# One level of Strassen for the first channel product of batches 5 to 7 and of the tail chunk

## The chip, the cores and the metric

The kernel runs on one core of one Trainium2 chip. Its time is the device time of one execution in microseconds (us); the median of three executions stands for it. A profile of one more execution shows what each engine did: TensorE (PE, and PEld for its weight loads), VectorE (DVE), ScalarE (ACT), GpSimd (POOL) and SyncE (SP), which here only issues transfers.

## The reference

The program is attention with random features, followed by a mixer with a token part and a channel part. Cut to its sums, for 8 batches, 8 heads, 576 tokens and 64 values per head:

```python
q_p, k_p = phi(q * scale), phi(k * scale)      # 128 features, exp of a projection
kv  = einsum('bhsm,bhsd->bhmd', k_p, v)
num = einsum('bhsm,bhmd->bhsd', q_p, kv)       # divided by the sum of the features
x   = attention as (8, 576, 512)
u   = x + (relu(x^T @ w_tok1) @ w_tok2)^T      # 576 -> 256 -> 576 tokens
out = u + relu(u @ w_ch1) @ w_ch2              # 512 -> 1536 -> 512 channels
```

The change concerns `u @ w_ch1`, called here the first channel product. `relu(...) @ w_ch2` is the second.

## The kernel before, in words

Of each batch the first 512 tokens are one chunk; the last 64 tokens of all eight batches are gathered into a ninth chunk, the tail, which is chunk number 8 in the code. For each batch the kernel loads q, k and v (from batch 2 on through a copy in DRAM and a transposing transfer on SP's queue), forms the features, the attention output `x`, and in the token part `u`. A transposing transfer then brings `u` into the layout `uT`, in which the channels lie on the partitions.

The channel part of a chunk is `channel_mix`. Its first product has 12 blocks of 128 hidden channels. For each, four matmuls of 512 columns (L966) sum over the 512 input channels in one of the eight PSUM banks, and one instruction, on ScalarE or VectorE, applies relu and writes `r3` as 16-bit floats (`relu_to`, L290 on ScalarE, L292 on VectorE). The second product is done from chunk 1 on by one level of Strassen's algorithm, in `channel_out_fast`: VectorE forms eight sums of quarters of `r3` (the tile `S`, `tt` at L295), TensorE computes seven products of 12 matmuls of 256 columns (L916) into three banks X, Y and Z that go on accumulating, and after each product VectorE reads a bank out and adds it to `u` or to what it read before (`read`, L905). Each of the seven products waits for the relus of all 12 blocks. The tail's second product is done in two halves, so that the last reads and stores are small.

The work is recorded as jobs with an engine, a planner's cost, dependencies, and buffers that they take and give back. `Planner.run` does not plan: it issues the jobs in an order written out in `ORDER`, with buffer places from `SLOT`, and `MOVED` overrides a job's usual engine by its number. So each engine's instructions stand in the sequence in which `ORDER` names them, and an instruction that must wait holds up all behind it on its engine. `engine(usual)` looks a job up in `MOVED`. The helper that applies a relu knows two engines:

```python
def relu_to(eng, out, in_):
    if eng == "ACT":
        nc.scalar.activation(out=out, in_=in_, func=AF.Relu)
    else:
        nc.vector.tensor_relu(out=out, in_=in_)
```

while `tt`, for sums of two tiles, has a branch for GpSimd. Rings of buffers: three each for transposed q, transposed k, v and `uT`, four each for the features `qp` and `kp`, two for `r3`, one for `S`, eight PSUM banks.

Of the kernel before, what the change touches and what calls it, by code (L numbers as in the profile page):

```python
# [81 lines left out]
]  # L82
SLOT = (
    "0100234050607011034025217063304156020014123024233037016112506321174115613214067030406102530471612141"
    "6710324016307250311067345122353640751421105324100325261073641220501046112501420700521173142350120702"
    "6123534100753141200127003221065413207102503410160022357312126034171542176210025011041121126022037516"
# [82 lines left out]
def kernel(  # L169
# [27 lines left out]
    R = SM // 2  # L197
    RT = ST // 2
    RA = R + RT
    NPE = 2  # L200
    RW = S * 4 // P
    c_scale = float(1.0 / math.sqrt(math.sqrt(D)))

# [93 lines left out]
    def bank(name):  # L297
        return banks[place("bank", name)]
# [772 lines left out]
```

## Time and profile before

| | us |
|---|---|
| median of the runs | 277.35 |
| lowest and highest | 276.93, 278.52 |
| span of the profiled execution, first to last instruction | 275.9 |
| TensorE busy in that span | 266.6 |
| VectorE busy | 222.9 |
| ScalarE busy | 138.1 |
| GpSimd busy | 91.2 |

The span leaves out what lies around the first and the last instruction, so the median stands 1.45 us above it. A row of a group shows line, engine, operation, output and input, shapes and count, then busy time and mean duration, then idle time before the group and what ended it. Instructions of one engine overlap a little in such rows: what a queue pays for an instruction is the distance between the starts of two that follow each other directly.

### The profile page before, as it was taken

To read this page: it belongs to the slowest core of one execution; us is meant where nothing else is said; L and a number is where in the kernel's file an instruction comes from. 1 tells how busy PE (TensorE), PEld (TensorE's weight loads), DVE (VectorE), ACT (ScalarE), POOL (GpSimd) and SP (SyncE) were. 2 spreads that over 40 slices of the span, in tenths; PEclk is the share of its full clock that TensorE was granted. 3 is DMA by queue.
4 is the path that set the end of the run, shared out by engine and by line. 5 is a ranking of instruction groups with operands and counts; after the bars stand their busy time and mean duration, and the time that the engine had idled before them with its cause. 6 is when DMAs were issued, how large, how long until landed. Compare 5 with 4: busy or idle time off the path is not lost.

```text
span 275.9 us, 6228 instructions
## 1 busy us (share of the span) xinstructions
PE 266.6 (97%) x2503; PEld 165.5 (60%) x2503; DVE 222.9 (81%) x462; ACT 138.1 (50%) x289; POOL 91.2 (33%) x115
## 2 busy tenths in 40 slices
PE   8789999999999999999999999999999999999993
PEld 3367455444567655755676656755676477446782
DVE  3897889876998799987999899978985992675992
ACT  3999941188685338734756456636654500040200
POOL 8994492063703490075019510600043000000001
PEclk9999999999999999999999999999999999999998
DMA  7999999999998999979989994840252304021125
GB/s 195 192 209 212 190 212 177 202 193 146 203 191 133 229 176 186 151 148 171 198 184 183 232 125 123 191 90 2 97 79 77 96 0 95 2 99 53 78 83 146
DMA packets 81292, 39.66 MB, mean 144 GB/s; under 512 B 63984, under 2 KB 77040, under 8 KB 81072
## 3 DMA queue, kind: packets, MB, share of 16 engines
q0 software_dynamic: 31744, 17.74, 44.2%
q1 hardware_dynamic: 47072, 15.50, 28.7%
q10 hardware_dynamic: 2448, 6.03, 5.6%
q8 instruction: 19, 0.31, 0.5%
q14 instruction: 9, 0.07, 0.1%
HBM read 35.95 MB, written 16.52 MB: 190 GB/s over the span
## 4 chain that ended last, share of the span: by engine, by line
PE 89%; DMA 6%; POOL 3%; DVE 0%; issue 0%; POOLq 0%
PE bank L966 33%; PE bank L916 25%; PE bank L777 5%; PE bank L790 5%; DMA w1m<-in_moe_w_tok_dram 4%; PE bank L1000 4%; PE bank L734 3%; PE bank L656 3%; PE bank L668 2%; PE bank L701 2%; DMA uT<-u 2%; POOL r L319 1%; PE bank L844 1%; PE bank L816 1%; PE bank L828 1%; PE bank L736 1%
## 5 line engine op out<-in xcount | busy, mean ns | idle before, releaser
L966 PE MATMUL bank<-uT,wc 128*128 128x512 f16 x376 | 90.4, 379 | 0.3 <-DMA uT<-u 0.3
L290 ACT ACTIVATE r<-bank 128x512 f16<-128x512 f32 (+1 forms) x84 | 46.9, 597 | 77.1 <-PE bank L966 62.0
L295 POOL TENSOR_TENSOR vs<-v,vs 128x512 f16<-128x512 f16 x31 | 33.2, 1074 | 91.2 <-DVE vs L682 60.5
L966 PEld LDWEIGHTS <-wc 128*128 128x128 f16 x424 | 38.3, 98 | 37.9 <-issue 1.1
L916 PEld LDWEIGHTS <-r 128*128 128x128 f16 x384 | 36.9, 98 | 8.1 <-issue 1.2
L514 ACT ACTIVATE kp<-bank 128x512 f16<-128x512 f32 x64 | 35.6, 622 | 10.4 <-PE bank L656 10.4
L514 ACT ACTIVATE qp<-bank 128x512 f16<-128x512 f32 x64 | 36.3, 616 | 8.9 <-PE bank L668 6.0
L680 DVE TENSOR_REDUCE km<-kp 128x8 f16<-128x1024 f16 x32 | 38.6, 1206 | 2.5 <-ACT kp L514 2.4
L292 DVE TENSOR_SCALAR r<-bank 128x512 f16<-128x512 f32 (+1 forms) x42 | 27.7, 672 | 12.0 <-PE bank L966 11.2
L744 DVE TENSOR_TENSOR x<-bank,rc 128x320 f16<-128x320 f32 x62 | 30.5, 492 | 2.1
L916 PEld LDWEIGHTS <-S 128*128 128x128 f16 x288 | 27.9, 98 | 5.4 <-issue 0.3
L905 DVE TENSOR_TENSOR o<-u,bank 128x512 f32<-128x512 f16 x28 | 19.0, 679 | 6.9 <-PE bank L916 6.8
L916 PE MATMUL bank<-T,r 128*128 128x256 f16 x192 | 23.8, 273 | 0.0
L916 PE MATMUL bank<-T,S 128*128 128x256 f16 x192 | 23.6, 273 | 0.0
L916 PE MATMUL bank<-wc,r 128*128 128x256 f16 x192 | 23.6, 273 | 0.0
L945 POOL DMA_DIRECT2D out_dram<-o x2 | 1.3, 648 | 60.9 <-issue 60.9
L793 DVE TENSOR_TENSOR u<-x,bank 128x512 f16<-128x512 f16 x28 | 17.8, 681 | 1.1 <-PE bank L790 1.0
L905 DVE TENSOR_TENSOR o<-o,bank 128x512 f32<-128x512 f32 (+1 forms) x27 | 16.6, 618 | 2.2 <-PE bank L916 1.6
L734 PEld LDWEIGHTS <-qp 128*128 128x128 f16 x256 | 13.8, 98 | 7.0 <-DVE kvsb L286 0.2
L734 PE MATMUL bank<-kvsb,qp 128*128 128x65 f16 x256 | 15.6, 193 | 0.0
L743 DVE RECIPROCAL rc<-bank 128x5 f32<-128x5 f32 x62 | 11.5, 186 | 4.1 <-PE bank L736 2.7
L701 PEld LDWEIGHTS <-kp 128*128 128x128 f16 x256 | 11.5, 98 | 5.1
(120 smaller groups left out, 376.3 us busy)
## 6 DMA issues: line engine op xcount, KB each, us to landing
out_dram<-o ACTq DMA_DIRECT2D x9, 512.0 KB, 2.6
q<-in_q_dram POOLq DMA_DIRECT2D x6, 576.0 KB, 7.2
wc<-in_moe_w_ch_dram POOLq DMA_DIRECT2D x4, 768.0 KB, 10.6
k<-in_k_dram POOLq DMA_DIRECT2D x6, 512.0 KB, 6.9
v<-in_v_dram POOLq DMA_DIRECT2D x6, 512.0 KB, 8.9
out_dram<-o SPq DMA_DIRECT2D x5, 512.0 KB, 3.9
r<-in_q_dram POOLq DMA_DIRECT2D x4, 288.0 KB, 7.3
v<-in_v_dram POOLq DMA_DIRECT2D x4, 256.0 KB, 8.7
```

The lines of the kernel that those rows point to most:

```text
L290: nc.scalar.activation(out=out, in_=in_, func=AF.Relu)
L292: nc.vector.tensor_relu(out=out, in_=in_)
L295: (nc.gpsimd if eng == "POOL" else nc.vector).tensor_tensor(**kw)
L514: nc.scalar.activation(out=out, in_=in_, func=AF.Exp, bias=0.0, scale=1.0)
L680: nc.vector.reduce_max(out=mx, in_=kpv, axis=AX.X)
L701: nc.tensor.matmul(ps[:, i, :], kpv[:, 2 * i + j // 2, j % 2, :], vs[:, i * NJ + j, 0 : D + 1], start=(i == 0 and j == 0), stop=False, ski ...
L734: nc.tensor.matmul(ps[:, k, j * 65 : (j + 1) * 65], st, s[:, i, 0 : D + 1], start=True, stop=True)
L744: nc.vector.tensor_tensor(out=t_x[place("x", b)][:, :, (2 * hp + hs[0]) * D : (2 * hp + hs[0] + n) * D].rearrange("p j (i d) -> p i j d", ...
L793: nc.vector.tensor_tensor(out=t_u[place("u", b)][:, j, :], in0=t_x[place("x", b)][:, j, :], in1=bank(n), op=ALU.add)
L905: nc.vector.tensor_tensor(out=o, in0=a, in1=ps, op=ALU.add)
L916: nc.tensor.matmul(ps[:, j * DH : (j + 1) * DH], a[:, cb, j * P : (j + 1) * P], w[:, cb, :], start=(bank_of(b, j0) not in held and j == j0 ...
L966: nc.tensor.matmul(ps, wc1[:, db, cb * P : (cb + 1) * P], moving(db), start=(db == 0), stop=(db == ND - 1))
```

## The change

For chunks 5, 6, 7 and 8 (`FAST_IN = 5`) `channel_in_fast` replaces the 12 blocks of the first product. The product is taken as 2 x 2 blocks (hidden channels by tokens, over two halves of the input channels) and computed by seven block products instead of eight. In three passes (`m` = 0, 1, 2), each over a third of the hidden channels, there are seven products of four matmuls of 256 columns in three banks:

- Once for all chunks, four sums of quarters of `w_ch1` (`weight_sums`, on GpSimd), kept in two places of the ring of transposed q and two of the ring of transposed k.
- Once per chunk, four differences of quarters of `uT` (on VectorE), kept in a place of the ring for v.
- In each pass: P1, P2 and P5 start banks X, Y and Z. ScalarE keeps the state of X three times (`keep`, a copy to 32-bit floats in a place of the `qp` or `kp` ring), between P1 and P6, P6 and P7, P7 and P4. VectorE adds a kept state to bank Y or Z three times (`join`, into `r3`). Three of the four blocks need relu after that: one instruction for two of them, `relu1` on 1024 values per partition, one for the third, `relu22` on 512 values, both in place in `r3`; the fourth is applied while bank X is read out (`relu21`).

`ORDER`, `SLOT` and `MOVED` are new. The sequence of real work is the same up to the second product of batch 2 (its product number 5), and all engines' sequences differ from there on; ahead of it only a few filler matmuls on zeros and the places of buffers differ. `MOVED` names GpSimd for eleven of the new relus (six `relu1`, five `relu22`). `relu_to` is unchanged, and in the built program none of them stands in GpSimd's sequence: these eleven stand in VectorE's, each at its place in `ORDER`.

```diff
+    def weight_sums(key):
+        def quad(i, k):
+            return wc1[:, 2 * k : 2 * k + 2, i * (DC // 2) : (i + 1) * (DC // 2)]
+        steps = ((quad(1, 0), quad(1, 1), ALU.add), (0, quad(0, 0), ALU.subtract), (quad(0, 0), quad(1, 0), ALU.subtract), (quad(0, 1), 1, ALU.subtract))
+        for i, (a, b, op) in enumerate(steps):
+            e_sum = engine("POOL")
...
+    def channel_in_fast(c, key, jt):
...
+        steps = ((lambda: block(0, 1), lambda: block(0, 0)), (lambda: block(1, 1), lambda: sums()[:, 0]), (lambda: block(1, 1), lambda: block(0, 1)),
+                 (lambda: block(1, 0), lambda: sums()[:, 1]))
...
+            def product(what, deps, m=m):
...
+                    for n in range(2):
+                        for a in range(2):
+                            nc.tensor.matmul(ps[:, n, :], w_[:, a, (2 * m + n) * P : (2 * m + n + 1) * P], x_[:, a],
+                                             start=(what in ("P1", "P2", "P5") and n == 0 and a == 0), stop=False, skip_group_check=True)
...
+            def keep(what, b, dep, m=m):
+                e_keep = engine("ACT")
+                def go(what=what, b=b, e_keep=e_keep, m=m, c=c):
+                    copy(e_keep, kept(what, m), bank(bank_of(b, m)))
...
+            def join(what, b, i, j, deps, free, m=m):
+                def go(what=what, b=b, i=i, j=j, m=m, c=c):
+                    nc.vector.tensor_tensor(out=r3(i, j, m), in0=kept(what, m).rearrange("p (n t) -> p n t", n=2), in1=pair(b, m), op=ALU.add)
...
+            p1 = product("P1", [])
+            p2 = product("P2", [])
+            p5 = product("P5", [])
+            k1 = keep("P1", "X", p1)
+            c11 = join("P1", "Y", 0, 0, [k1, p2], True)
+            p6 = product("P6", [k1])
+            k2 = keep("U2", "X", p6)
+            p7 = product("P7", [k2])
+            k3 = keep("U3", "X", p7)
+            c22 = join("U3", "Z", 1, 1, [k3, p5], False)
+            p3 = product("P3", [c22])
+            c12 = join("U2", "Z", 0, 1, [k2, p3], True)
+            p4 = product("P4", [k3])
+            e_relu = engine("ACT")
+            def relu21(e_relu=e_relu, m=m, c=c):
+                relu_to(e_relu, r3(1, 0, m), pair("X", m))
...
+            e_relu = engine("DVE")
+            def relu1(e_relu=e_relu, m=m, c=c):
+                t = t_r3[place("r3", c)][:, 2 * m : 2 * m + 2, :]
+                relu_to(e_relu, t, t)
...
+            e_relu = engine("DVE")
+            def relu22(e_relu=e_relu, m=m, c=c):
+                relu_to(e_relu, r3(1, 1, m), r3(1, 1, m))
...
     def channel_mix(c, key, jt):
...
+        if c >= FAST_IN:
+            channel_out_fast(c, key, channel_in_fast(c, key, jt))
+            return
...
+        if b == FAST_IN:
+            weight_sums(b - 1.0)
         channel_mix(b, float(b), uT)
```

More of the change, by code (lines that the diff above doesn't have):

```diff
@@ L100 @@
[L100 to L103 removed]
+    44: "ACT", 48: "ACT", 53: "ACT", 61: "ACT", 64: "ACT", 67: "ACT", 68: "ACT", 114: "DVE", 116: "ACT",
@@ L104 @@
+    857: "ACT", 858: "POOL", 873: "POOL", 874: "POOL", 897: "ACT", 1003: "ACT", 1004: "POOL", 1019: "POOL",
+    1020: "ACT", 1035: "POOL", 1036: "ACT", 1059: "ACT", 1060: "ACT", 1166: "DVE", 1168: "POOL", 1182: "DVE",
+    1184: "ACT", 1199: "POOL", 1200: "ACT", 1223: "ACT", 1224: "ACT", 1247: "POOL", 1248: "ACT", 1264: "ACT",
+    1278: "DVE", 1279: "ACT", 1280: "POOL", 1318: "SP", 1323: "ACT", 1324: "SP", 1325: "ACT", 1326: "SP",
 }
@@ L200 @@
     NPE = 2
+    FAST_IN = 5
     RW = S * 4 // P
@@ L865, in channel_out_fast @@
             part = slice(g * NH // 2, (g + 1) * NH // 2)
-            need = [jr[cb + NH * e] for cb in range(part.start, part.stop) for e in range(2)]
+            need = [x for cb in range(part.start, part.stop) for e in range(2) for x in jr[cb + NH * e]]
             steps = (
@@ L953, in channel_out_fast, with sum_of, go @@
             dma(eng, key + 0.9 + 0.1 * i, 1.3, store, deps=[outs[x, 0] for x in need], give=[("o", (c, i))], cost=0.4)
+    j_sums = []
+    def sum_of(i):
+        return (t_qT if i < 2 else t_kT)[place("qT" if i < 2 else "kT", ("sum", i))][:, 0 : 2 * DC // 2].rearrange("p (a c) -> p a c", a=2)
+    def weight_sums(key):
[4 more added lines that the diff above has]
+            e_sum = engine("POOL")
+            def go(i=i, a=a, b=b, op=op, e_sum=e_sum):
+                a, b = [sum_of(x) if isinstance(x, int) else x for x in (a, b)]
+                tt(e_sum, out=sum_of(i), in0=a, in1=b, op=op)
+            need = [j_sums[x] for x in (a, b) if isinstance(x, int)]
+            j_sums.append(add(e_sum, 3.0, key, go, deps=[*need, *j_wc1], take=[("qT" if i < 2 else "kT", ("sum", i))]))
@@ new lines, in channel_in_fast, with block, sums, go @@
+    def channel_in_fast(c, key, jt):
+        def block(k, j):
+            return (t_uT[place("uT", c)] if c < B else uTt)[:, 2 * j : 2 * j + 2, 2 * k : 2 * k + 2, :].rearrange("p j a t -> p a j t")
+        def sums():
+            return t_v[place("v", ("sums", c))].rearrange("p h e -> p (h e)").rearrange("p (i a j t) -> p i a j t", i=4, a=2, j=2)
+        steps = ((lambda: block(0, 1), lambda: block(0, 0)), (lambda: block(1, 1), lambda: sums()[:, 0]), (lambda: block(1, 1), lambda: block(0, 1)),
+                 (lambda: block(1, 0), lambda: sums()[:, 1]))
+        j_s = []
+        for i, (a, b) in enumerate(steps):
+            e_sum = engine("DVE")
+            def go(i=i, a=a, b=b, e_sum=e_sum, c=c):
+                tt(e_sum, out=sums()[:, i], in0=a(), in1=b(), op=ALU.subtract)
+            j_s.append(add(e_sum, 0.35, key, go, deps=[*jt, *([j_s[i // 2]] if i % 2 else [])], take=[("v", ("sums", c))]))
+        half_c = DC // 2
+        def weights(i, k):
+            return lambda: wc1[:, 2 * k : 2 * k + 2, i * half_c : (i + 1) * half_c]
+        ops = {
+            "P1": ("X", weights(0, 0), lambda: block(0, 0), []),
+            "P2": ("Y", weights(0, 1), lambda: block(1, 0), []),
+            "P5": ("Z", lambda: sum_of(0), lambda: sums()[:, 0], [j_sums[0], j_s[0]]),
+            "P6": ("X", lambda: sum_of(1), lambda: sums()[:, 1], [j_sums[1], j_s[1]]),
+            "P7": ("X", lambda: sum_of(2), lambda: sums()[:, 2], [j_sums[2], j_s[2]]),
+            "P4": ("X", weights(1, 1), lambda: sums()[:, 3], [j_s[3]]),
+            "P3": ("Z", lambda: sum_of(3), lambda: block(1, 1), [j_sums[3]]),
+        }
+        jr = [[] for _ in range(NCB)]
+        for m in range(NH // 2):
+            kk = key + 0.5 * m / 3
+            def bank_of(b, m=m):
+                return ("in" + b, c, m)
+            def pair(b, m=m):
+                return bank(bank_of(b, m)).rearrange("p (n t) -> p n t", n=2)
+            def product(what, deps, m=m):
+                b, w, x, need = ops[what]
+                used = [("qT" if i < 2 else "kT", ("sum", i)) for i in range(4) if what == ("P5", "P6", "P7", "P3")[i]]
+                def go(b=b, w=w, x=x, what=what, m=m, c=c):
+                    ps, w_, x_ = pair(b, m), w(), x()
+                    for n in range(2):
+                        for a in range(2):
+                            nc.tensor.matmul(ps[:, n, :], w_[:, a, (2 * m + n) * P : (2 * m + n + 1) * P], x_[:, a],
+                                             start=(what in ("P1", "P2", "P5") and n == 0 and a == 0), stop=False, skip_group_check=True)
+                j = add("PE", mm(4, 256), kk, go, deps=[*need, *jt, *j_wc1, *deps], take=[("bank", bank_of(b))], give=[("v", ("sums", c)), *used] + ([("uT", c)] if c < B else []))
+                j.heavy = True
+                return j
+            def part(what, m=m):
+                tag = "qp" if (what == "U2") == (m % 2 == 0) else "kp"
+                return tag, (what, c, m)
+            def kept(what, m=m):
+                tag, name = part(what, m)
+                t = t_qp[place(tag, name)].rearrange("p a b -> p (a b)") if tag == "qp" else t_kp[place(tag, name)].rearrange("p a b e -> p (a b e)")
+                return t.bitcast(FP32)
+            def keep(what, b, dep, m=m):
+                e_keep = engine("ACT")
+                def go(what=what, b=b, e_keep=e_keep, m=m, c=c):
+                    copy(e_keep, kept(what, m), bank(bank_of(b, m)))
+                return add(e_keep, 0.5, kk, go, deps=[dep], take=[part(what)])
+            def r3(i, j, m=m):
+                return t_r3[place("r3", c)][:, NH * i + 2 * m : NH * i + 2 * m + 2, 2 * P * j : 2 * P * j + 2 * P]
+            def join(what, b, i, j, deps, free, m=m):
+                def go(what=what, b=b, i=i, j=j, m=m, c=c):
+                    nc.vector.tensor_tensor(out=r3(i, j, m), in0=kept(what, m).rearrange("p (n t) -> p n t", n=2), in1=pair(b, m), op=ALU.add)
+                return add("DVE", 0.6, kk, go, deps=deps, take=[("r3", c)], give=[part(what)] + ([("bank", bank_of(b))] if free else []))
+            p1 = product("P1", [])
[14 more added lines that the diff above has]
+                relu_to(e_relu, r3(1, 0, m), pair("X", m))
+            c21 = add(e_relu, 0.5, kk, relu21, deps=[p4], take=[("r3", c)], give=[("bank", bank_of("X"))])
+            e_relu = engine("DVE")
+            def relu1(e_relu=e_relu, m=m, c=c):
+                t = t_r3[place("r3", c)][:, 2 * m : 2 * m + 2, :]
+                relu_to(e_relu, t, t)
+            c1 = add(e_relu, 0.35, kk, relu1, deps=[c11, c12], take=[("r3", c)])
+            e_relu = engine("DVE")
+            def relu22(e_relu=e_relu, m=m, c=c):
+                relu_to(e_relu, r3(1, 1, m), r3(1, 1, m))
+            c2 = add(e_relu, 0.2, kk, relu22, deps=[c22], take=[("r3", c)])
+            for n in range(2):
+                jr[2 * m + n] = [c1]
+                jr[NH + 2 * m + n] = [c21, c2]
+        return jr
@@ L984, in relu @@
                 relu_to(e_relu, t_r3[place("r3", c)][:, cb, :], bank(n))
-            jr[cb] = (add(e_relu, 0.5, key + 0.5 * pos / NCB, relu, deps=[j1], take=[("r3", c)], give=[("bank", n)]))
+            jr[cb] = [add(e_relu, 0.5, key + 0.5 * pos / NCB, relu, deps=[j1], take=[("r3", c)], give=[("bank", n)])]
         if fast:
@@ L1001, in channel_mix @@
                 prev = add("PE", mm(4, 512) + (mm(4, P) if part == 2 else 0.0), key + 0.5 + 0.5 * (3 * j + part) / 12, c2,
-                           deps=[prev, *jr[4 * part : 4 * part + 4], *j_wc2], take=[("bank", n)], give=[("r3", c), ("uT", c)])
+                           deps=[prev, *(x for done in jr[4 * part : 4 * part + 4] for x in done), *j_wc2], take=[("bank", n)], give=[("r3", c), ("uT", c)])
             k2 = key + 0.5 + 0.5 * (3 * j + 3) / 12
```

33 lines of the change are left out of this document (14 added, 19 removed), and 123 rows, old and new, of the table ORDER.

## The prediction

> **What bounds the kernel now.** I read the page first, then the chain of waits in order of time, then busy time by stretches.
>
> ```profile
> span 275.9 us, 6228 instructions
> ...
> PE 266.6 (97%) x2503; PEld 165.5 (60%) x2503; DVE 222.9 (81%) x462; ACT 138.1 (50%) x289; POOL 91.2 (33%) x115
> ...
> PE 89%; DMA 6%; POOL 3%; DVE 0%; issue 0%; POOLq 0%
> ```
>
> The chain is TensorE for 89% of the span, and VectorE for 0% of it, though VectorE is the second busiest. In the chain by time, the stretch that the new order covers begins with the second product of batch 2, at 131.39:
>
> ```profile
> 131.39 1.31 PE bank L916 x12
> ...
> 234.09 13.81 PE bank L966 x64
> ...
> 260.94 10.51 PE bank L916 x96
> 271.48 0.42 DVE o L905
> ```
>
> A matmul of 512 columns costs 13.81/64 = 0.216 us, one of 256 columns 10.51/96 = 0.1095. After the last of them there remain VectorE's last read, to 271.90, and 4.0 us of stores, to 275.9. By stretches (columns: PE, PEld, DVE, ACT, POOL busy, then clock and transfers):
>
> ```profile
> 131.40:271.90 140.50, 140.04 (x1202) 91.37 (x1200) 114.86 (x232) 56.78 (x114) 23.55 (x26) 1.00 0.50 105
> 131.40:160.00 28.60, 28.60 (x289) 18.72 (x288) 26.24 (x57) 16.61 (x35) 11.76 (x14) 1.00 1.08 195
> 160.00:190.00 30.00, 30.00 (x275) 18.21 (x274) 27.22 (x56) 16.33 (x33) 5.29 (x6) 1.00 0.62 117
> 219.00:248.00 29.00, 29.00 (x179) 17.16 (x178) 19.12 (x33) 5.04 (x10) 0.00 (x0) 1.00 0.17 43
> ```
>
> TensorE has no gap at full clock. VectorE is busy 114.86 of 140.5 us, so it has 25.6 us to spare; in the first two rows only about 2.5 of 29. This spare time is what the change spends.
>
> **TensorE's part.** Per chunk 48 x 0.216 = 10.36 us become 7 products x 3 passes x 4 matmuls x 0.1095 = 9.20. That is 1.16 us less, for four chunks 4.7 us. If all else stays hidden, the span is 271.2.
>
> **VectorE's part.** Prices per instruction are distances between starts:
>
> ```profile
> L292 DVE TENSOR_SCALAR r<-bank 128x512 f16<-128x512 f32 x23 | 15.4, 686 | 8.8 <-PE bank L966 8.5
> ```
> ```profile
> 210.15 0.68 DVE L905 TENSOR_TENSOR o<-o,bank 128x512 f32<-128x512 f32 x1
> 210.75 0.68 DVE L905 TENSOR_TENSOR o<-u,bank 128x512 f32<-128x512 f16 x1
> ```
> ```profile
> 104.28 0.55 DVE L295 TENSOR_TENSOR S<-r 128x768 f16<-128x768 f16 x1
> ...
> 107.47 0.55 DVE L295 TENSOR_TENSOR S<-S,r 128x768 f16<-128x768 f16 x1
> ```
> ```profile
> 48.17 0.95 DVE L448 TENSOR_TENSOR T<-wc 128x1536 f16<-128x1536 f16 x1
> 49.04 0.95 DVE L448 TENSOR_TENSOR T<-wc,T 128x1536 f16<-128x1536 f16 x1
> ```
>
> ```profile
> 265.87 0.41 DVE L905 TENSOR_TENSOR o<-ut,bank 128x256 f32<-128x256 f16 x1
> 266.20 0.41 DVE L905 TENSOR_TENSOR o<-o,bank 128x256 f32<-128x256 f32 x1
> ```
>
> An instruction that reads 512 values from a bank costs 0.60 (210.15 to 210.75), one that reads 256 costs 0.33 (265.87 to 266.20). The six steps from 104.28 to 107.47 give 0.53 for a sum of 768 16-bit values, at best 0.47; 1536 values cost 0.87. From 0.47 and 0.87: 0.52 ns per value and 0.07 us fixed, so 0.34 for 512 values and 0.60 for 1024.
>
> Out go 22 of the 23 relus from banks that VectorE does in this stretch: 22 x 0.60 = 13.2. In come 36 joins (a bank of 512 plus 512 32-bit values, the form of the row at 210.15): 36 x 0.60 = 21.6. Sixteen differences of `uT`, 512 values: 16 x 0.34 = 5.4. Three `relu21` from a bank: 1.8. Nine `relu1` of 1024 values and five `relu22` of 512, eleven of these fourteen being those that `MOVED` gives to GpSimd and `relu_to` issues on VectorE. A relu inside SBUF has no row. Upper end: the price of a sum of two tiles, 0.60 and 0.34. Lower end: the fixed part and half of the rest, 0.34 and 0.20. I take 0.52 and 0.33, nearer the upper end, whose rows are nearest: 6.3 in all, between 4.1 and 7.1. The sum: 114.9 - 13.2 + 21.6 + 5.4 + 1.8 + 6.3 = 136.8 us (134.6 to 137.6), against 140.5 - 4.7 = 135.8 for TensorE. The spare time is gone, and VectorE becomes the longer engine of the stretch.
>
> By the tier table in the Trainium skill's "VectorE: DVE Perf Modes" (The perf-mode tier table), a 16-bit single-source instruction inside SBUF runs at four values per cycle, a sum of two tiles at two. With that page's errata formula, an estimate is 0.33 us for `relu1` and 0.19 for `relu22`; VectorE's sum would be 134.4, and the time below 278.8 instead of 280.0 (four and three of them lie ahead of the point that counts). No run here shows such an instruction yet.
>
> **The other engines.**
>
> ```profile
> 101.66 2.63 ACT L290 ACTIVATE r<-bank 128x512 f16<-128x512 f32 x5 [4.29 <-PE bank L966]
> ```
> ```profile
> L295 POOL TENSOR_TENSOR vs<-v,vs 128x512 f16<-128x512 f16 x31 | 33.2, 1074 | 91.2 <-DVE vs L682 60.5 <-PE bank L668 22.3 <-PE bank L966 4.5
> ...
> L295 POOL TENSOR_TENSOR T<-vt,T 128x1024 f16<-128x1024 f16 x1 | 1.9, 1941 | 0.0
> ```
>
> ScalarE pays (2.63 - 0.60)/4 = 0.51 per bank. It gets 36 keeps (18.4) and 19 new relus, three of them on 1024 values (about 11.2), and loses 26 (13.3): 56.8 + 16.3 = 73 of 140, not a bound. GpSimd: 0.87 us per 512 values more, so 2.8 for a sum of 1536; four make 11.2, and 23.6 becomes 35. They stand in front of its multiplications for batches 6 and 7; `kv` of batch 6 comes some 10 us after the third sum in TensorE's order, so that cover holds. Cost: nothing.
>
> Transfers: two of the three places for transposed q now hold sums, so batch 7's q loads only when batch 6's is used up, and on SP it stands behind a store of batch 4.
>
> ```profile
> uT<-u SPq DMA_TRANSPOSE x7, 5.4
> ...
> qT<-q SPq DMA_TRANSPOSE x6, 6.1
> ```
>
> By my count of the sequences it lands 1 us before TensorE needs it. Cost nothing, no more cover than that.
>
> **On the path.** I follow the new sequences from 131.4. Batch 6's second product waits for all relus of its first; the last is a `relu1` on VectorE. Behind it in VectorE's order stand 18 joins (10.8), 24 sums S (12.7), 14 reads of 0.60 (8.4), 14 half reads of 0.33 (4.6), 8 differences (2.7), 10 relus (5.1) and an addition (0.6): 44.9. So ahead of it are 136.8 - 44.9 = 91.9. VectorE also waits ahead of it: about 0.5 for batch 5's `uT` (5.4 us after the last addition to `u`), 0.5 at the start, and 1.4 where P5, join, P3, join follow each other across two engines (P3 alone is 4 x 0.1095 = 0.44, and three times VectorE has nothing ready beside it): 2.4, an estimate from walking through the two sequences side by side with these prices; its ends are 0 and 5. TensorE is free about 1.7 us before the relu ends and waits.
>
> Behind the relu TensorE has seven products of 1.31 (9.2), 42 first products of batch 7 and the tail at 0.44 (18.4), seven of 1.31 for batch 7 (9.2) and 84 matmuls for the tail (9.2): 46.0. There it waits about 2.0 more: 0.5 for the five relus in a row on VectorE ahead of batch 7's second product, 0.8 for that one's sums S (with a `relu22` just ahead of them), 0.7 around the tail, whose seven joins and three relus follow each other on VectorE.
>
> Sum: 131.4 + 91.9 + 2.4 + 0.1 (hand-over) + 46.0 + 2.0 = 273.8 for the last matmul; 0.2 until its result can be read, 0.45 for the read (271.45 to 271.90 before) and 4.0 for the stores give a span of 278.5, 2.6 more than 275.9. The median of the runs stood 1.45 above that span: 277.35 + 2.6 = **280.0 us**.
>
> **The rivals.**
> 1. Faster: VectorE runs without a gap. VectorE's spare time so far (25.6 us) speaks for buffers that let it run ahead. Against it: joins sit between matmuls in both directions. With no waits at all, the span is 278.5 - 4.4 = 274.1, the median 275.6; with the lower price of the relus (1.1 less ahead of batch 6's last relu) 274.5. It decides once the waits fall below 0.4 us, or 1.5 with cheap relus.
> 2. No change: half of the waits. 280.0 - 2.2 = 277.8; with cheap relus 276.7. VectorE then gives back just what TensorE saves.
> 3. Slower still: GpSimd's sums of 1536 values hold up VectorE's sums of two tiles. One of them can meet each of the S sums or the differences for up to 2.8 us, and VectorE has nothing left to hide that; one or two such meetings give 282.8 to 285.6. In the rows from 219 on GpSimd has no sum at all, so the trace doesn't decide it. The Trainium skill's "SBUF — State Buffer" (SBUF: two separate sides) states such a rule: a VectorE instruction with two SBUF inputs and a GpSimd one that reads SBUF lock a shared pair of ports for the whole instruction. No run here shows it.
>
> **How the numbers follow.** No change means within 0.5%, 1.4 us, about what a measurement of this kernel can tell. Chances: rival 1 0.12, rival 2 0.25, the forecast (278.7 to 282) 0.43, rival 3 0.20. So faster 0.12, same 0.25, slower 0.63. The range leaves out most of rival 1 and the upper part of rival 3: 275.8 to 284; slower cases alone: 278.7 to 285.6.
>
> **What would show it.** In the new profile, between 131 and 272 us: VectorE's busy time near 137 us against 115; TensorE's near 136 with gaps, which end on joins, relus or reads by VectorE; VectorE in the chain with some per cent, where it had 0%. A `relu1` lasting 0.35 us instead of 0.6 would show rival 2's price. A VectorE sum that lasts 1 us or more beside a GpSimd sum shows rival 3. The prediction is wrong if TensorE stays without gaps behind batch 5, which needs VectorE to run joins well ahead of need, or if TensorE waits at batch 7's q.

## The result and the profile after

The changed kernel takes 289.12 us (median; 288.40 to 292.81), the kernel before in the same runs 277.3: the ratio is 1.0421, with an interval of 1.0396 to 1.0445. The forecast was 280.0, with a range of 275.8 to 284.0. The sign was right, the size was not: 11.8 us more instead of 2.6. An execution more than 1.5% above the fastest of its kernel and at a lower clock, like the one of 292.81 us here, counts in the medians but not in the ratios, so differences between variants of the change are taken from the ratios below (1% is 2.8 us). The profile shown here is of one more execution, which took 288.34 us at a span of 286.6. Its page, then its busy time by stretches (columns as before: PE, PEld, DVE, ACT, POOL, then clock, share of the transfers, GB/s):

```profile
span 286.6 us, 6599 instructions
...
PE 268.8 (94%) x2647; PEld 182.0 (64%) x2647; DVE 247.0 (86%) x506; ACT 155.9 (54%) x321; POOL 104.5 (36%) x119
...
PE 57%; DVE 20%; DMA 9%; issue 7%; POOL 3%; ACT 2%; POOLq 0%; DVEq 0%
```
```profile
131.00:160.00 29.00, 27.33 (x304) 18.09 (x302) 25.52 (x55) 19.75 (x41) 16.93 (x15) 1.00 1.12 198
160.00:190.00 30.00, 24.77 (x219) 17.04 (x216) 27.43 (x46) 14.14 (x29) 12.59 (x9) 0.89 0.42 75
190.00:220.00 30.00, 29.08 (x300) 22.09 (x298) 29.29 (x58) 18.83 (x38) 5.83 (x5) 1.00 0.32 78
```

VectorE is now in the chain with 20%, and between 190 and 220 us it is busy 29.29 of 30 us: this is what was forecast. What was not forecast lies in the first two rows. Between 160 and 190 us TensorE is busy for 24.77 us only, at a granted clock of 0.89. Its waits from 128 us on (total, times, longest), and its rows around the first of the seven products of batch 4's second channel product:

```profile
PE bank L922 <- DVE r L298: 5.3, 2, 4.6
PE bank L557 <- DMA kT<-k: 1.7, 1, 1.7
```
```profile
169.92 0.62 PE L850 MATMUL bank<-r,w 128*64 128x512 f16 x4 [0.31 <-DVE u L799]
175.19 2.72 PE L922 MATMUL bank<-wc,r 128*128 128x256 f16 x12 [4.65 <-DVE r L298]
177.70 0.64 PE L707 MATMUL bank<-vs,kp 128*128 128x65 f16 x8
...
180.57 0.29 PE L740 MATMUL bank<-kvsb,qp 128*128 128x65 f16 x4
```

Three losses stand here. TensorE waits 1.67 us at 141.90 for transposed k of batch 6. It waits 4.65 us for batch 4's last relu. And behind that its first 12 matmuls take 2.51 us (175.19 to 177.70) where 1.31 is the price at full clock. Why the relu is late is seen in VectorE's rows ahead of it and GpSimd's rows beside them:

```profile
161.93 2.61 DVE L599 TENSOR_TENSOR vbd<-rct,mask 128x8 f16<-128x8 f16 x1
...
169.78 1.39 DVE L301 TENSOR_TENSOR S<-r 128x768 f16<-128x768 f16 x1
171.21 3.32 DVE L301 TENSOR_TENSOR r<-r 128x768 f16<-128x768 f16 x1
174.46 0.68 DVE L298 TENSOR_SCALAR r<-bank 128x512 f16<-128x512 f32 x1
```
```profile
160.36 3.11 POOL L301 TENSOR_TENSOR kT<-wc,qT 128x1536 f16<-128x1536 f16 x1
163.43 1.06 POOL L301 TENSOR_TENSOR vs<-v,vs 128x512 f16<-128x512 f16 x1
...
167.68 3.08 POOL L301 TENSOR_TENSOR vs<-v,vs 128x512 f16<-128x512 f16 x3 [1.37 <-DVE vs L688]
170.72 3.40 POOL L301 TENSOR_TENSOR kT<-wc 128x1536 f16<-128x1536 f16 x1
```

A product of 8 values per partition lasts 2.61 us beside GpSimd's third sum and the multiplication behind it (0.20 us elsewhere); a sum of two tiles lasts 3.32 us beside the fourth sum, another 1.39 beside three multiplications (0.55 elsewhere). Together that is some 6 us, and it is the sign that the prediction named for rival 3. VectorE's reduces and its reads of banks between them keep their times. GpSimd's first two sums, at 152.39 and 155.58, meet no VectorE instruction on two tiles, and nothing is late there.

In the kernels below the list of jobs takes another number of lines, so that the same line has another number: L301 (L295 in the kernel before) is L286 in most variants of the changed kernel and L281 in those of the kernel before.

### The profile page after: what moved, and what is told of

The parts are those of the page before. It is cut to its first block, busy times and chain, and to the rows that moved or that the text cites. A ratio compares the mean times of both kernels' runs of the same rounds, so it can differ in the third digit from the quotient of the medians.

```text
span 291.0 us, 6599 instructions
## 1 busy us (share of the span) xinstructions
PE 271.0 (93%) x2647; PEld 183.2 (63%) x2647; DVE 249.1 (86%) x506; ACT 155.8 (54%) x321; POOL 104.6 (36%) x119
## 4 chain that ended last, share of the span: by engine, by line
PE 58%; DVE 21%; issue 8%; DMA 5%; ACT 5%; POOL 0%; POOLq 0%; DVEq 0%
PE bank L1086 14%; PE bank L922 14%; PE bank L1018 7%; PE bank L1120 4%; DMA kT<-k 3%; DVE km L686 3%; DVE S L301 3%; DVE r L1039 3%; DVE o L911 3%; PE bank L707 2%; PE bank L740 2%; DVE u L799 2%; PE bank L783 2%; DMA uT<-u 2%; PE bank L662 2%
## 5 line engine op out<-in xcount | busy, mean ns | idle before, releaser
L301 POOL TENSOR_TENSOR vs<-v,vs 128x512 f16<-128x512 f16 x31 | 33.1, 1072 | 79.9 <-DVE vs L688 40.0
L1086 PE MATMUL bank<-uT,wc 128*128 128x512 f16 x232 | 56.2, 379 | 1.8 <-DVE o L911 1.8
L296 ACT ACTIVATE r<-bank 128x512 f16<-128x512 f32 (+1 forms) x67 | 38.1, 596 | 34.5 <-PE bank L1086 19.0
L922 PEld LDWEIGHTS <-r 128*128 128x128 f16 x384 | 37.7, 100 | 15.2 <-issue 7.4
L1086 PEld LDWEIGHTS <-wc 128*128 128x128 f16 x232 | 20.9, 98 | 22.3 <-issue 3.1
L922 PE MATMUL bank<-wc,r 128*128 128x256 f16 x192 | 25.7, 290 | 4.9 <-DVE r L298 4.5
L922 PE MATMUL bank<-T,S 128*128 128x256 f16 x192 | 24.9, 282 | 0.5 <-DVE o L911 0.3
L292 ACT CAST kvsb<-bank 128x130 f16<-128x130 f32 x23 | 6.7, 293 | 22.1 <-PE bank L714 18.7
L292 ACT COPY qp<-bank 128x512 f32<-128x512 f32 x16 | 9.4, 587 | 15.8 <-PE bank L1018 11.0
L292 ACT COPY kp<-bank 128x512 f32<-128x512 f32 x20 | 11.0, 594 | 12.5 <-PE bank L1018 12.5
L298 DVE TENSOR_SCALAR r<-bank 128x512 f16<-128x512 f32 (+1 forms) x23 | 15.0, 659 | 3.1 <-PE bank L1086 2.6
## 6 DMA issues: line engine op xcount, KB each, us to landing
wc<-in_moe_w_ch_dram POOLq DMA_DIRECT2D x4, 768.0 KB, 11.2
```

The source lines that it names most:

```text
L292: (nc.scalar.copy if eng == "ACT" else nc.vector.tensor_copy)(out=out, in_=in_)
L301: (nc.gpsimd if eng == "POOL" else nc.vector).tensor_tensor(**kw)
L922: nc.tensor.matmul(ps[:, j * DH : (j + 1) * DH], a[:, cb, j * P : (j + 1) * P], w[:, cb, :], start=(bank_of(b, j0) not in held and j == j0 ...
L1086: nc.tensor.matmul(ps, wc1[:, db, cb * P : (cb + 1) * P], moving(db), start=(db == 0), stop=(db == ND - 1))
```

## The experiments

**1. The changed kernel again, the sums on VectorE, transposed k later, and both.** The edits are in the written-out lists alone (where the order changes, the places in `SLOT` follow it):

```diff
 MOVED
+    819: "DVE", 820: "DVE", 821: "DVE", 822: "DVE",
 ORDER
-    744, 907, 752, 682, 909, 583, 742, 743, 905, 586, 768, 1063, 584, 795, 908,
+    744, 752, 682, 583, 742, 743, 905, 586, 768, 1063, 584, 795,
...
-    783,
+    783, 907, 909, 908,
```

> The changed kernel once more, for its profile and as the measure of the runs beside it. Both theories: 288 to 289.5 us, and in the profile the same three marks between 131 and 190 us: TensorE waits 2.5 us for transposed k of batch 6, VectorE's sums of two tiles last 1.4 to 3.9 us where GpSimd's sums of weights run beside them (0.55 elsewhere), and TensorE waits 3.8 us for the last relu of batch 4 and then runs at a granted clock of 0.8 to 0.9 for some 10 us.

> The four sums of weights stand in VectorE's sequence instead of GpSimd's, at the same places of the order. Theory A (a GpSimd sum holds up VectorE's sums of two tiles for as long as it runs): the four stretched sums lose 1.1 + 3.4 + 0.85 + 2.8 = 8.2 us, VectorE pays 4 x 0.87 = 3.5 for the sums, so 288.9 - 4.7 = 284.2 us; if TensorE's clock then stays up behind the shorter wait, up to 2 less: 282 to 284.5. Theory B (VectorE simply has too much work there, and the long sums are long for another reason, such as late data): the sums of two tiles keep their 1.4 to 3.9 us, and the time rises by up to 3.5, to 289 to 292.4.

> The transposed k of batch 6 (a matmul group and its two exps) moves some 14 matmul groups later in the order, to about where it stood before the change. Theory C (this wait is a loss of its own): TensorE's wait of 2.5 us goes, and with it the low clock behind it (0.76 for 7 us, about 1.7 us): 284.7 us, 284 to 287. Rival D (VectorE, held up at 151 to 158 us, decides that stretch anyway, so the wait had cover): the time stays at 288 to 289.5, and TensorE waits by so much more for VectorE's sums and reads at 150 to 160 us.

> Both edits in one. Theories A and C: 288.9 - 4.7 - 2.5 = 281.7 us, and with the clock up in the whole stretch 278 to 282. If A holds with rival D: as with the sums moved alone, 282 to 284.5. If B: not below 287. Should it come out at 279 to 281, these two causes are the whole gap between the forecast of 280.0 and the 289 measured.

| | median, us | ratio to before, with interval |
|---|---|---|
| the change again | 288.89 | 1.0419 (1.0367 to 1.0471) |
| sums on VectorE | 286.07 | 1.0320 (1.0275 to 1.0365) |
| transposed k later | 287.81 | 1.0371 (1.0323 to 1.0419) |
| both | 285.75 | 1.0304 (1.0257 to 1.0351) |

With the sums on VectorE the product with the mask is back at 0.20 us, and no sum of two tiles lasts over 1.4. The gain is 2.7 us rather than 4.7: VectorE pays for the sums in the stretch where it is late, and TensorE waits 1.3 us for one of them. Moving k gave 1.3 us instead of 4.2, and the intervals overlap, so this is not clear of the noise: TensorE's wait for it is gone, but the wait for the relu still is 4.2 us. So rival D is nearer there: most of that loss had cover, as long as the sums held VectorE up. Both edits together leave 5.7 us above the forecast. Two causes were seen, but neither edit removes its cause cleanly.

**2. One part alone: the sums in the kernel before.** Four sums of weights go into GpSimd's sequence of the kernel before, behind job 879; a second kernel writes zeros there, a third copies.

```diff
+            x, y = [wc1[:, 2 * k : 2 * k + 2, h * (DC // 2) : (h + 1) * (DC // 2)] for h, k in (a, c2)]
+            tt("POOL", out=uTt.rearrange("p a b c -> p (a b c)")[:, 0:DC].rearrange("p (k n) -> p k n", k=2), in0=x, in1=y, op=op)
+        add("POOL", 3.0, 5.0, go)
```

In the kernel with zeros, and in the one with copies, the middle line is:

```diff
+            for _ in range(2):
+                nc.gpsimd.memset(uTt.rearrange("p a b c -> p (a b c)")[:, 0:DC].rearrange("p (k n) -> p k n", k=2), 0.0)
```
```diff
+            nc.gpsimd.tensor_copy(out=uTt.rearrange("p a b c -> p (a b c)")[:, 0:DC].rearrange("p (k n) -> p k n", k=2), in_=x)
```

> One part of the change alone: the kernel before, with four sums of 1536 values of the weights on GpSimd behind its multiplication for batch 6's tail, at 160.4 us, written to a tile that holds nothing yet (nobody reads them). GpSimd is idle there until 172.5, and VectorE's eight sums S of batch 4 (0.55 us each, 161.1 to 166) fall into it. Theory A (a GpSimd sum with two inputs in SBUF and a VectorE sum with two inputs in SBUF exclude each other for the whole instruction): about four of the eight S sums last 2 to 3.5 us, VectorE is 6 to 10 us late, of which the 2 us of spare time that it has there hide little: 281 to 287 us. Rival B (GpSimd's sums cost VectorE nothing): 277, all S sums at 0.55.

> The same places, but GpSimd only writes zeros there, eight times 1536 values, and reads nothing. Theory A in its strict form (it is GpSimd's reading that excludes VectorE): 277 us and S sums at 0.55. If GpSimd's writing alone is enough, or any work of GpSimd: S sums of 1 us and more beside it, and 278 to 284.

> The kernel before with four copies of 1536 values inside SBUF on GpSimd at the place where the four sums cost 10.7 us: one input instead of two. If one input read from SBUF is enough to exclude VectorE's products of two tiles: these last as long as the copy beside them (1.5 to 3 us), 280 to 286 us. If it takes two inputs: 277, sums S at 0.55.

The sums alone cost the kernel before 10.7 us, more than expected: 287.70 against 276.96, ratio 1.0372 (1.0334 to 1.0410). VectorE's rows, GpSimd's, and TensorE's wait:

```profile
160.15 2.45 DVE L281 TENSOR_TENSOR S<-r 128x768 f16<-128x768 f16 x1
162.52 0.68 DVE L278 TENSOR_SCALAR r<-bank 128x512 f16<-128x512 f32 x1
163.30 2.66 DVE L281 TENSOR_TENSOR S<-r 128x768 f16<-128x768 f16 x1
165.88 3.43 DVE L281 TENSOR_TENSOR r<-r 128x768 f16<-128x768 f16 x1
169.24 3.43 DVE L281 TENSOR_TENSOR S<-S,r 128x768 f16<-128x768 f16 x1
172.60 0.55 DVE L281 TENSOR_TENSOR r<-r 128x768 f16<-128x768 f16 x1
```
```profile
159.09 13.17 POOL L281 TENSOR_TENSOR uTt<-wc 128x1536 f16<-128x1536 f16 x4
```
```profile
PE bank L902 <- DVE o L891: 8.9, 1, 8.9
```

Four of VectorE's sums each wait for GpSimd for 1.9 to 2.9 us, where one GpSimd sum takes 3.3; the relu between them, which reads a bank, keeps its 0.68. With zeros, which GpSimd writes for 11.43 us in the same place, the time is 277.36, ratio 1.0003 (0.9983 to 1.0022), and the same sums stay at 0.55:

```profile
162.51 0.55 DVE L281 TENSOR_TENSOR r<-r 128x768 f16<-128x768 f16 x1
162.98 0.55 DVE L281 TENSOR_TENSOR S<-S,r 128x768 f16<-128x768 f16 x1
```
```profile
159.44 11.43 POOL L1025 MEMSET uTt<- 128x1536 f16 x8
```

With copies (1.67 us each) the time is 284.47 us (two executions, ratio 1.0241, 1.0144 to 1.0339). VectorE's sums again wait, 1.81 us twice, and TensorE 2.2 us for them. That run was 5 us late already ahead of the copies (it had waited 4.2 us for a transposed k at 82.82), so only its rows are read, not its time:

```profile
168.37 1.81 DVE L281 TENSOR_TENSOR r<-r 128x768 f16<-128x768 f16 x1
```

So it is shown that GpSimd's reading from SBUF, with one input or two, holds up VectorE's instructions on two tiles in SBUF, each for up to about one GpSimd instruction here, and that writing alone does not. This is the rule of the Trainium skill, "SBUF — State Buffer" (SBUF: two separate sides): the one that starts first has the shared ports for its whole instruction. The rows of this experiment agree with it; some that do not follow so simply stand in the last section.

**3. The price of the low clock.** Sixteen matmuls that nobody reads fill TensorE's wait for batch 4's last relu in the changed kernel; they stand in the order as -10, sixteen times, ahead of job 715.

```diff
+        if i >= 8:
+            nc.tensor.matmul(banks[i - 8], wc1[:, 0, 0:P], wc1[:, 0, 0:512], start=True, stop=True)
+            return
```

> The changed kernel with 16 matmuls of 512 columns on weights into a free bank (3.45 us at full clock, read by nobody) ahead of the first product of batch 4's second product, where TensorE waits 4.4 us. Theory E (the low clock of 0.66 behind that wait is set by TensorE having been idle, and costs time of its own: from 175.19 to 180.57 the sequence takes 5.38 us, the same sequence at full clock 3.21 in the run with both edits): 288.9 - 2.2 = 286.7 us, 286 to 287.5, clock 1.0 in 170 to 180. Rival F (VectorE sets the pace behind it, so the slow matmuls had cover): clock 1.0, but 288.5 to 289.5.

286.48 us; ratio to before 1.0343 (1.0294 to 1.0392), which is 2.1 us below the change's 1.0419 and clear of its first executions too (1.0396 to 1.0445). From 170 to 180 us, the change first:

```profile
170.00:180.00 10.00, 5.35 (x41) 3.90 (x41) 9.78 (x13) 3.37 (x8) 4.12 (x2) 0.66 0.63 125
```
```profile
170.00:180.00 10.00, 8.37 (x66) 4.50 (x64) 9.82 (x12) 3.66 (x9) 6.45 (x4) 1.00 0.65 125
```

The granted clock is 1.00 instead of 0.66, and the sequence that took 5.38 us (175.19 to 180.57) takes 3.22 (177.53 to 180.75). Theory E holds: the wait costs its length and some 2 us more, since the clock falls in this wait and is low for the first rows behind it. Work that does nothing made the kernel faster.

**4. No meetings, first with zeros.** In the changed kernel GpSimd writes zeros in place of the four sums, with transposed k later and without.

```diff
-                tt(e_sum, out=sum_of(i), in0=a, in1=b, op=op)
+                nc.gpsimd.memset(sum_of(i), 0.0)
```

> Transposed k later, and GpSimd writes zeros in place of the four sums (so P3, P5, P6 and P7 are computed from zeros). Theory A: GpSimd reads nothing there, so no sum of VectorE lasts over 0.6 us beside it, but for those beside its multiplications; this is the change with sums at no cost, which the forecast assumed: 279.5 to 282.5 us. If it stays at 285 or more, the sums explain less than half of the gap and the forecast's sum of VectorE's work or of the waits is wrong as well.

> The changed kernel with GpSimd writing zeros in place of the four sums (so P3, P5, P6 and P7 are computed from zeros), and transposed k where the change has it. If the sums are the larger part of the gap and k's wait is a loss of its own: 281.1 + 1.7 = 282.8 us, 282 to 284. If k's wait only hides behind the sums (no cost of its own once they are gone): 281 to 281.6. If the two need each other (with k's wait, other meetings or the low clock return): 285 or more.

Zeros with k later: 281.12 us, 1.0131 (1.0105 to 1.0158). Zeros alone: 284.32, 1.0220 (1.0171 to 1.0270). The page of the first:

```profile
span 278.7 us, 6597 instructions
...
PE 266.6 (96%) x2647; PEld 180.9 (65%) x2647; DVE 241.8 (87%) x506; ACT 155.7 (56%) x321; POOL 97.2 (35%) x119
```

The span is 278.7; the forecast's was 278.5. This is the kernel that the forecast described, though the agreement is in part luck (see below). The gap above it divides in two ways: from the change's 1.0419 the sums' reading first takes off 5.5 us and the k step then 2.5, or k first 1.3 and the reading then 6.7. The two overlap, and both orders give 8.0. Each of these four numbers is uncertain by 1.5 to 2 us.

**5. No meetings, with the real sums.** There are three attempts to place the sums where VectorE has no instruction on two tiles. Jobs 819, 820, 822 and 821 are the four sums in the order of time, 910 is VectorE's group with the product with the mask. Each line shows a job behind its new neighbour in the order. The first placing, run without and with k later:

```diff
+    949, 910,
+    822, 821,
```

The second, with k later (and with the places in the ring of transposed k that follow from it), and the third, with k later:

```diff
+    820, 822,
+    1062, 821,
```
```diff
 ORDER
+    820, 822,
+    714, 821,
 MOVED
+    821: "DVE",
```

> The changed kernel with two steps moved in the order and nothing else. VectorE's group for batch 6's tail (a reduce, a reciprocal and the product with the mask, the one that lasted 2.61 us beside GpSimd's third sum) goes ahead by one reduce and some reads, between GpSimd's second and third sum; GpSimd's fourth sum goes directly behind the third, where VectorE reduces and adds out of banks, and away from the sums S. Theory A (only the meetings cost, not the sums): 2.4 + 2.8 us of holds and the low clock behind them (2.2 us) go; a sum S may still wait 1 to 1.5 us for GpSimd's three multiplications, which come 3 us later: 281.5 to 284 us, sums S at 0.55 but for one or two. Rival I (GpSimd has become the late one: its multiplications for batch 6, 3 us later, hold up TensorE): 285 to 288, with TensorE's wait on vs of 2 us or more.

> The same, and transposed k of batch 6 later. Theories A and C: 1.7 us less than with the placing alone, 280 to 282.5 us; if it is 279 to 282, the forecast's 280.0 was right but for the meetings, the moved step and the clock. Rival I: 284 to 287.

> The changed kernel with transposed k later and with GpSimd's third sum directly behind the first two, its loads of k behind that, then the fourth sum, then its multiplications for batch 6; VectorE's order as in the change. By the times of the run with zeros, GpSimd then sums from 150.8 to 160.1 and from 161.8 to 164.9, and VectorE has no instruction with two inputs in SBUF there but the product with the mask at 161.0, between the two. Theory A (only meetings cost): 281 to 283.5 us, no VectorE product over 1.5 us. If sums on GpSimd cost time without meeting anything (by the lateness of its multiplications, say): 285 to 288. If the product with the mask is met again, it lasts up to 3 us and the time is 284 to 286.

> The changed kernel with transposed k later, three of GpSimd's sums in a row from 151 to 160.2 us, where VectorE reduces and reads banks, and the fourth on VectorE behind the sums S of batch 4 (0.87 us). Nothing is left out. Theory A (only meetings cost): no product of VectorE over 1.5 us, 281.1 + 0.9 = 282 us, 281 to 283.5. If the three sums cost without a meeting: 284 to 288, with TensorE waiting for GpSimd.

The first placing was slower than the change (291.24 us, 1.0493, interval 1.0461 to 1.0525), with k later it was 288.59 (1.0407, 1.0373 to 1.0441), the second 288.70 (1.0383, 1.0320 to 1.0445). All three still had a meeting with the smallest instruction there is (and the first placing without k later one with a sum S, which lasted 3.92 us). VectorE and GpSimd in the first placing with k later:

```profile
159.98 6.00 DVE L584 TENSOR_TENSOR vbd<-rct,mask 128x8 f16<-128x8 f16 x1
```
```profile
159.80 3.09 POOL L286 TENSOR_TENSOR kT<-wc,qT 128x1536 f16<-128x1536 f16 x1
162.85 3.08 POOL L286 TENSOR_TENSOR kT<-wc 128x1536 f16<-128x1536 f16 x1
```

Eight values per partition waited out two sums in a row, and TensorE waited 6.5 us for what came behind them. It came 0.18 us behind the start of the third sum, where I had expected it ahead of it, and this was enough. The third placing has no meeting with a sum:

```profile
161.54 0.20 DVE L584 TENSOR_TENSOR vbd<-rct,mask 128x8 f16<-128x8 f16 x1
```
```profile
151.35 3.11 POOL L286 TENSOR_TENSOR qT<-wc 128x1536 f16<-128x1536 f16 x1
...
157.72 3.09 POOL L286 TENSOR_TENSOR kT<-wc,qT 128x1536 f16<-128x1536 f16 x1
```

It takes 282.29 us (282 was expected), ratio 1.0202 (1.0155 to 1.0249), with nothing left out. So the three sums of 3.1 us cost nothing that can be measured where they meet nothing, and this version is 6.0 us faster than the change, though still slower than the kernel before.

**6. What is left: VectorE's amount of work?** Three kernels take the eleven relus, named for GpSimd and standing on VectorE, away: to ScalarE on top of both edits of experiment 1, to ScalarE on top of zeros with k later, and out of the kernel on top of the same. A fourth puts them on ScalarE in the first placing.

```diff
+    841: "ACT", 858: "ACT", 873: "ACT", 874: "ACT", 1004: "ACT", 1019: "ACT", 1035: "ACT", 1168: "ACT", 1199: "ACT", 1247: "ACT", 1280: "ACT",
```

and where they are left out (`relu22` likewise):

```diff
-                relu_to(e_relu, t, t)
+                if e_relu != "POOL":
+                    relu_to(e_relu, t, t)
```

> Sums of weights on VectorE, transposed k later, and the eleven relus that were named for GpSimd and stand on VectorE now go to ScalarE. Theory G (with the holds gone, VectorE's amount of work sets the time, as the forecast had it): VectorE loses six relus of 1024 values at 0.38 and five of 512 at 0.19, 3.3 us; 285.75 - 3.3 = 282.4 us, 281.5 to 284. Rival H (what is left is a chain of waits between engines, and ScalarE takes longer for each of these relus): 285 to 287, with TensorE's waits now ending on ScalarE.

> Zeros in place of the sums, transposed k later, and the eleven relus on ScalarE instead of VectorE. Theory G (VectorE's amount of work, 44 of 44 us busy with few gaps, sets what is left above the kernel before): 281.1 less 2 to 3.3: 277.8 to 279.1. Rival H (what is left are handovers between engines): 280.5 to 282, and TensorE's waits ending on ScalarE's relus in place of VectorE's.

> As with zeros in place of the sums and transposed k later, and the eleven relus that were named for GpSimd are left out (those blocks of the hidden layer keep their negative values). Theory G (VectorE's amount of work sets what is left): six times 0.35 and five times 0.2 us less, 3.1, so 281.1 - 3.1 = 278.0 us, 277.5 to 279. Rival H (handovers between the engines set it, a relu more or less on VectorE has cover): 280 to 281.2.

> The same, and the eleven relus on ScalarE. Theory G (VectorE's amount of work then sets the time): 2 to 3.3 us less, 277 to 280. Rival H (chains of waits between the engines): as with placing and transposed k, within 1 us, with TensorE's waits ending on ScalarE or GpSimd.

Given to ScalarE they bring nothing that can be measured: 287.15 us on both edits (ratio 1.0311, 1.0250 to 1.0372, against 1.0304; TensorE there waits 2.5 us for GpSimd, whose v landed up to 20.2 us after its issue, against 11.4 with the relus on VectorE), 288.24 in the placing (1.0383, 1.0349 to 1.0416), and 280.64 with zeros (1.0102, 1.0069 to 1.0134, against 1.0131), where TensorE waits for ScalarE's features instead (1.2 us at batch 7's k). Left out they give 280.07 (1.0107, 1.0057 to 1.0157), at the lower edge of H's range. But the executions spread from 279.02 to 282.41, over both ranges, and the profiled one, the slowest, shows one reason; VectorE's row, then TensorE's:

```profile
167.22 3.68 DVE L286 TENSOR_TENSOR S<-r 128x768 f16<-128x768 f16 x1
```
```profile
172.14 2.33 PE L907 MATMUL bank<-wc,r 128*128 128x256 f16 x12 [2.95 <-DVE r L283]
...
177.14 0.60 PE L1003 MATMUL bank<-uT,wc 128*128 128x256 f16 x4
```

A sum S stands beside GpSimd's three multiplications and lasts 3.68 us (1.40 with the relus, in the run with zeros), then TensorE's clock is low. The way from there to the first matmul of the new first product takes 5.00 us; in the run with both edits of experiment 1 the same sequence takes 3.37 (172.79 to 176.16). Behind that point the kernel without relus is the shorter one: from 172.14 to the end of its span (280.6) are 108.5 us, less 1.6 for the clock 106.8; with the relus, at full clock, from 169.06 to 278.7, 109.6. That is 2.8 of the 3.1 us that theory G expected. It suggests that VectorE's work counts in the second half, but it is one execution of each, with the clock's share worked out, and the times do not show it. A relu moved to ScalarE only changes whom TensorE waits for.

## Why the prediction was wrong

By its own steps:

- **TensorE's part: right.** A product of four matmuls takes 0.44 us and one of 12 takes 1.31 at full clock (with zeros and k later, 256.18 to 256.62 and 257.93 to 259.24); there is no hidden price in the new products.
- **VectorE's part: right but for the relus.** Joins cost 0.60, as forecast (rows below). The relus inside SBUF were mis-sized: `relu1` takes 0.33 to 0.37 between starts and `relu22` 0.20 to 0.21, against 0.52 and 0.33. For nine and five of them that is 2 us too much. The estimates from the Trainium skill's "VectorE: DVE Perf Modes" (The perf-mode tier table), 0.33 and 0.19, were the better ones. By the pages VectorE's busy time grew by 18.9 us with zeros in place of the sums (222.9 to 241.8) where 21.9 were forecast, most of the difference being this. VectorE's rows of the changed kernel:

```profile
227.27 0.42 DVE L298 TENSOR_SCALAR r<-r 128x1024 f16<-128x1024 f16 x1
227.64 1.28 DVE L1039 TENSOR_TENSOR r<-kp,bank 128x512 f16<-128x512 f32 x2
228.84 1.28 DVE L1039 TENSOR_TENSOR r<-qp,bank 128x512 f16<-128x512 f32 x2
...
232.05 0.29 DVE L298 TENSOR_SCALAR r<-r 128x512 f16<-128x512 f16 x1
232.25 1.28 DVE L799 TENSOR_TENSOR u<-x,bank 128x512 f16<-128x512 f16 x2
```

- **"Four make 11.2 [...] Cost: nothing": the step that failed.** It looked for cover in TensorE's order, that is, at who waits for the sums, and not at whom the sums hold up. They cost 5.5 to 6.7 us. Rival 3 had the mechanism and named the S sums; it gave it 0.20 and at most 5.6 us. Its price was low in three ways: a sum takes 3.1 to 3.4 us instead of 2.8; a meeting can last longer than the sum, since the next GpSimd instruction follows without a pause (161.93 to 164.54 above, where the sum ends at 163.47); and one of the meetings was with a product of 8 values, which the rival did not think of. And the trace before the change was not silent on it. From 100 us on, two of VectorE's sums and products of two tiles run beside a GpSimd instruction there, both of them this small product. The first of them lasted until GpSimd's multiplication was over, 0.46 us instead of 0.19; the second, which began just ahead of the end of one, 0.23. The sums S never met one:

```profile
119.10 0.46 DVE L593 TENSOR_TENSOR vbd<-rct,mask 128x8 f16<-128x8 f16 x1
```
```profile
118.46 1.06 POOL L295 TENSOR_TENSOR vs<-v,vs 128x512 f16<-128x512 f16 x1 [0.34 <-DVE vs L682]
```

- **Transposed k of batch 6: not counted at all.** The prediction followed batch 7's q, which was no problem. The order also moves k's step ahead of three products of batch 3. In the kernel before, TensorE came to it at 145.16, 8.5 us after the transfer was issued; now it comes at 140.2, 6.9 us after the issue:

```profile
136.69 3.68 SPq L380 DMA_TRANSPOSE kT<-k  x1
```
```profile
145.16 0.29 PE L551 MATMUL bank<-omT,kT 64*128 64x128 f16 x4
```
```profile
133.34 6.32 SPq L386 DMA_TRANSPOSE kT<-k  x1
```
```profile
141.90 0.29 PE L557 MATMUL bank<-omT,kT 64*128 64x128 f16 x4 [1.67 <-DMA kT<-k]
```

  The first and second row are of the kernel before, the others of the change. The earlier place is one half of it: the transfer also landed 8.5 us after its issue, where it had landed after 6.1, which would have been in time. Why it takes longer stays open; with k later it takes 8.5 us again, and nobody waits for it. The wait costs 2.5 us without the sums' holds; beside them, the 1.3 us is not clear of the noise.
- **The waits on the path, 4.4 us: too low, and covered by luck.** With zeros in place of the sums and k later, TensorE begins batch 6's second product at 225.99 us, where 225.8 was forecast, and takes 47.8 us from there to the end of its last matmul, where 48.0 was forecast. But ahead of that point VectorE is busy for 89.9 of 94.5 us and idle for 4.6, where 91.9 and 2.4 were forecast: less work met more idle time. Even that work holds meetings that no step priced, of sums with GpSimd's own multiplications (1.40, 0.82 and 1.29 us at 166.42, 200.02 and 200.87, instead of 0.55). In the change itself a long wait cost more than its length: some 2.1 us went to the low clock.
- **The span of 278.5: what the kernel does without the two failed steps** (278.7), with the luck just named. The median stands 2.4 above that span instead of the 1.45 that were added; 0.6 of this is that the profiled execution, at 280.53 us, was the fastest. Rivals 1 and 2 would have needed spare time of VectorE, and it is not there: even without the sums' reading and with k later the change is 1.3% slower than before.

## What to carry to other kernels

Before work goes to GpSimd, look at VectorE's instructions on two tiles in SBUF that run beside it, down to the smallest: each can lose a whole GpSimd instruction or two, so a long GpSimd instruction belongs where VectorE reduces or reads PSUM. When an order is found anew, go through every step that waits on a transfer, not only through the steps that the change is about. A wait of TensorE of some microseconds can cost more than its length, and matmuls that nobody reads can be cheaper than an idle array.

## What the hardware showed that was not expected

- How long a VectorE instruction is held varies with the same neighbours: beside three GpSimd multiplications in a row a sum S lasted 1.40, 1.75 or 3.68 us in three kernels of the same order there. Whether it takes its turn behind the first or the last of them is not explained by these runs.
- In the second placing the product with the mask began at 162.08, 0.95 us before the sum that it then waited for, while GpSimd was issuing loads (161.29 to 163.02), and lasted 4.12 us. Whether the issuing held it was not tried.
- A relu inside SBUF, with a single input, lasted 0.82 us instead of 0.42 once, at 194.04 with zeros and k later, beside GpSimd's multiplications at 193.51 and 194.53. One row does not show a cause.
- The clock falls after shorter waits than I had expected. In the kernel with the fillers, TensorE's rows after its wait for transposed k show it:

```profile
142.89 0.40 PE L542 MATMUL bank<-omT,kT 64*128 64x128 f16 x4 [2.04 <-DMA kT<-k]
143.22 2.74 PE L907 MATMUL bank<-wc,r 128*128 128x256 f16 x12
145.75 1.72 PE L907 MATMUL bank<-T,S 128*128 128x256 f16 x12
```

  Twelve matmuls take 2.53 us here (143.22 to 145.75) instead of 1.31, about half rate, behind a wait of 2.04 us. It was low behind 2.95 and 4.65 us too, and not behind 1.67, 1.92 and 2.84; behind 1.88 us it was low in one kernel, where four shorter waits stood just ahead, and not in another. Between 1.9 and 3 us these runs give no rule.
